# One block and one product for the last 64 query rows of two head groups, without the idle products between stages

## The chip, the cores and the metric

The kernel runs on one core of a Trainium2 chip. The metric is the device time of one execution in microseconds (us). Three runs of the kernel before took 212.29, 211.98 and 211.97 us, so its median is 211.98 us. One further execution was profiled.

## The reference, cut to what matters

Four rows `x` of 448 numbers pass a decode step of attention over a window of 1024 cached positions, and then a small mixer:

```
q = (layernorm(x) @ wq)               # wq: 448 x 4096, 16 query heads of 256, 8 key/value heads
p = softmax(q @ k^T / 16)             # k, v: 4 x 8 x 1024 x 256 of the caches
h = x + (p @ v) @ wo                  # wo: 4096 x 448
y = layernorm(layernorm(h))
out = h + gelu(y @ w1 + b1) @ w2 + b2 # w1: 448 x 1792, w2: 1792 x 448
```

All is float32. Caches and weights are each read once, some 88 MB. The change touches the query projection `layernorm(x) @ wq`: its contraction over 448 rows is three blocks of 128 rows and a last one of 64.

## The kernel before, in words

A *group* is one key/value head with its two query heads (512 columns of `wq`); there are eight groups, handled in four pairs. The host packs everything that a stage needs into one array of 128 partitions, and one long load brings it into a slot. There are three slots, used in turn: the slots hold `wq0` and `k0` (one slot), then `l1` to `l8`, then the end (`k7`, `vo`, `v7`, `wo`, `w1`, `w2`). All loads are issued by SyncE (SP) in program order. A load into a slot waits for the last reader of the part that it overwrites, so SP stands between loads and waits for TensorE (PE). `Machine.emit` (lines 131 to 177) writes the waits out: all operations are recorded by one helper, line 74, so the rows of the profile mostly show line 74 and have to be told apart by tiles.

Names in the rows: `slot` is a slot, `qT`, `pT`, `oT`, `yT`, `gT` are small transposed operands, and `b_s`, `b_o`, `b_m`, `b_t`, `b_acc` are banks of PSUM for scores, values, small products, transposes and the running output. A float32 product shows as two MATMUL instructions, each with its own LDWEIGHTS; a bfloat16 product as one.

For a pair of groups the stages are: `both_queries` (line 493: projection of both groups into `b_m`, then `queries` transposes the result into `qT`), `scores`, `softmax`, `transpose_p`, `values`, `outputs`. The work of one pair is spread over several loads.

The projection, `project` (line 323), takes its parts from `wq_parts` (line 239). Its result is a bank in which quadrant `j` (32 partitions) takes the product with block `j` of the 448 rows; `queries` adds the four quadrants up later. Operand `yT[g]` holds the normalized rows so that group 0 comes out in rows 0 to 3 of a quadrant and group 1 in rows 4 to 7. Blocks 0 to 2 are 128 rows by 512 columns. The last 64 rows of a group are packed as 128 partitions by 256 columns (first half of the columns above, second half below), so quadrant 3 takes two products of half width per group:

```
for i in range(2):
    parts.append((3, y[:, 3 + i, :], slice(i * 2 * P, (i + 1) * 2 * P), t[:, 3 * 512 :]))
```

Group 1 of the first pair is an exception: its last 64 rows come in a tile of their own, `wq1_last` (64 partitions by 512 columns), by two small loads whose source has eight rows of 2 KB times four (lines 463 to 466):

```
for i in range(2):
    nc.sync.dma_start(
        wq1_last[i * Q : (i + 1) * Q, :], wq1[i].rearrange("e (p c) -> e p c", c=512)[:, :4, :]
    )
```

In SP's order they stand behind `wq0` and `k0` and ahead of `l1`.

At the end of seven stages `keep_warm_between` (line 444) issues six products of a tile of zeros, `idle` (bfloat16, 128 x 512), into a bank `b_t` that nothing reads. Similar calls of `keep_warm` stand in the tail, behind `l8`, and stay.

Of the kernel before, what the change touches and what calls it, by code (L numbers as in the profile page):

```python
# [5 lines left out]
F32 = mybir.dt.float32  # L6
# [5 lines left out]
B, D = 4, 448  # L12
HQ, HKV, SK, DH = 16, 8, 4096, 256
# [3 lines left out]
P = 128  # L17
H = P // 2
ND = 4
# [3 lines left out]
Q = 32  # L23
CACHE = NKC * B * DH
HALF = CACHE // 2
WEIGHTS = 4 * D
SLOT = CACHE + 2 * WEIGHTS + HALF
COLUMNS = ND * B + 4 + 4 * 4
EPS = 1e-5
# [2 lines left out]
GRANULE = 4  # L32


class Memory:
# [9 lines left out]
    def part(self, ap):  # L45
        if self.psum:
            return slice(0, 1), np.zeros(1, int)
        pairs = list(ap.ap)
        first, at = divmod(ap.offset, self.row)
        rows = slice(first // GRANULE, -(-(first + pairs[0][1]) // GRANULE))  # L50
        cols = np.zeros(1, int)
        for step, n in pairs[1:]:
            cols = (cols[:, None] + step * np.arange(n)).ravel()
        return rows, np.unique(cols) + at
# [142 lines left out]
        return flat.rearrange(f"p ({names}) -> p {names}", **{f"a{i}": n for i, n in enumerate(shape[1:])})  # L197


def block_kernel(nc, wq0, k0, wq1, l1, l2, l3, l4, l5, l6, l7, l8, k7, vo, v7, wo, w1, w2, out):  # L200
    real, nc = nc, Machine(nc)

    def rows_of_tag(name, shape, dtype):
# [13 lines left out]
    ps_s, ps_t, ps_m = (Pool(bank, 2) for _ in range(3))  # L217
    ps_o, ps_w = (Pool(bank, 1) for _ in range(2))

    def slot(name):  # L220
        return ring.tile([P, SLOT], F32, tag="slot", name=name)

    def load(t, at, src, pieces=None):
        dst = t[:, at : at + src.shape[-1]]
        at = 0
        for n in pieces or (src.shape[-1],):
            nc.sync.dma_start(dst[:, at : at + n], src[:, at : at + n])
            at += n
        return dst

    def cut(t, sizes):
        parts, at = [], 0
        for n in sizes:
            parts.append(t[:, at : at + n])
            at += n
        return parts


    def wq_parts(y, t, last=None):
        parts = [(a, y[:, a, :], slice(0, 512), t[:, a * 512 : (a + 1) * 512]) for a in range(3)]  # L240
        if last is not None:
            return parts + [(3, y[:H, 3, :], slice(0, 512), last)]
        for i in range(2):
            parts.append((3, y[:, 3 + i, :], slice(i * 2 * P, (i + 1) * 2 * P), t[:, 3 * 512 :]))
        return parts


    def keys(t):
# [2 lines left out]
    def chunks(t):  # L251
        v = t.rearrange("p (c b d) -> p c b d", b=B, d=DH)
        return [v[:, c : c + 2] for c in range(0, v.shape[1], 2)]

    def output_weights(t):
# [6 lines left out]
        out=ident, in_=ident, compare_op=ALU.not_equal, fill=1.0, base=0, pattern=[[-1, P]], channel_multiplier=1  # L262
# [9 lines left out]
    nc.vector.tensor_add(sel, sel, ident[:, 3 * Q : 4 * Q])  # L272


    yz = const.tile([P, ND + 1, B + Q], F32, name="yT")
    nc.vector.memset(yz, 0.0)
    yT = [yz[:, :, B:], yz[:, :, :Q]]
    wq1_last = const.tile([H, 512], F32, name="wq1_last")
    zT = const.tile([P, ND, Q], F32, name="zT")
    nc.vector.memset(zT, 0.0)  # L280

# [38 lines left out]
        nc.gpsimd.tensor_tensor(dst, ve, mhalf[: dst.shape[0], : dst.shape[1]], op=ALU.pow)  # L320


    def project(pq, parts, start):
        for j, y, cols, w in parts:
            nc.tensor.matmul(
                pq[j * Q : (j + 1) * Q, cols], y, w,
                start=start and cols.start == 0, stop=not start and cols.stop == 512,
            )

    def pq_tile(n):  # L330
        return ps_m.tile([P, 512], F32, tag="m", name=f"pq{n}")

    def queries(n, pq):
        qs = work.tile([P, 512], F32, tag="qs", name=f"qs{n}")
        nc.scalar.copy(qs, pq)

        pt = ps_m.tile([P, 2 * REP, P], F32, tag="m", name=f"pqt{n}")
        for i in range(2 * REP):
            nc.tensor.transpose(pt[:, i, :], qs[:, i * P : (i + 1) * P], ident)
        sm = work.tile([P, 2 * REP, 2 * B], F32, tag="sm", name=f"sm{n}")  # L340
        nc.vector.tensor_reduce(
            sm, pt.rearrange("p i (j q) -> p i q j", j=4)[:, :, : 2 * B, :], axis=AX.X, op=ALU.add
        )
        for g in range(2):
            src = sm.rearrange("p (r c) b -> p c b r", r=REP)[:, :, g * B : (g + 1) * B, :]
            for i in range(2):
                at = (2 * g + i) * REP
                nc.vector.tensor_copy(qT[g][:, :, :, at : at + REP], src)
# [91 lines left out]
    def keep_warm(n, warm):  # L440
        for _ in range(n):
            nc.tensor.matmul(warm[:Q], idle[:, :Q], idle, start=True, stop=True)

    def keep_warm_between():
        warm = ps_t.tile([P, 512], F32, tag="t", name="between")
        keep_warm(6, warm)

    def po_tile(g, pool=ps_o, tag="o"):
        return pool.tile([P, 2, DH], F32, tag=tag, name=f"po{g}")


    t = slot("t0")
    wqt, xT, b2T, b1T = cut(load(t, 0, wq0), (WEIGHTS, ND * B, 4, 4 * 4))
    wqt = wq_parts(yT[0], wqt)
    xT = xT.rearrange("p (a b) -> p a b", a=ND)
    ka, kb, wqt1 = cut(load(t, WEIGHTS + COLUMNS, k0), (HALF, HALF, 3 * 512))
    for i in range(2):
        nc.sync.dma_start(
            wq1_last[i * Q : (i + 1) * Q, :], wq1[i].rearrange("e (p c) -> e p c", c=512)[:, :4, :]
        )  # L460
    d = work.tile([P, ND, B], F32, tag="d", name="d_x")
    centred(d, xT, "x")
    sx = work.tile([P, ND, B], F32, tag="sx", name="sx")
# [1 line left out]
    rx = work.tile([P, B], F32, tag="rx", name="rx")  # L465
    rsqrt(rx, column_mean(sx, "sx"), "x")
    nc.vector.tensor_mul(yT[0][:, :3, :B], d[:, :3, :], rx[:, None, :].to_broadcast([P, 3, B]))
    nc.vector.tensor_mul(yT[0][:H, 3, :B], d[:H, 3, :], rx[:H, :])
    nc.vector.tensor_mul(yT[0][H:, 4, :B], d[H:, 3, :], rx[H:, :])
    pq = pq_tile(0)  # L470
    project(pq, wqt, True)

    wide = t[:, SLOT - 6 * P :].rearrange("p (n j q) -> p n j q", n=6, j=4)
    nc.vector.tensor_copy(
# [5 lines left out]
    for at, n in ((0, 2), (2 * P, 4)):  # L480
# [3 lines left out]
        cols = min(n * P, rs.shape[1] - at)  # L484
        nc.scalar.copy(rs[:, at : at + cols], pr.rearrange("p i c -> p (i c)")[:, :cols])

    project(pq, wq_parts(yT[1], wqt1, wq1_last), False)
    queries(0, pq)
    s = score_tiles(0)
    for h, kt in enumerate((ka, kb)):  # L490
# [2 lines left out]
    def both_queries(n, wqs):  # L493
        pq = pq_tile(n)
        for g in range(2):
            project(pq, wq_parts(yT[g], wqs[g]), g == 0)
        queries(n, pq)

    def outputs(n, po, rec, wos):
        transposed_output(n, po, rec, range(2))  # L500
        for g in range(2):
            add_output(n, g, output_weights(wos[g]))

    ka, kb, va = cut(load(slot("l1"), 0, l1), (HALF, HALF, HALF))
    for h, kt in enumerate((ka, kb)):
        scores(s, 1, h, keys(kt))
    p, sums = softmax(0, s)
    rec = transpose_p(0, p, sums)
    po = po_tile(0)
    values(0, chunks(va), po, range(0, 2))  # L510
    keep_warm_between()

    vb, v, wo_a, wo_b = cut(load(slot("l2"), 0, l2), (HALF, CACHE, WEIGHTS, WEIGHTS))
    values(0, chunks(va) + chunks(vb), po, range(2, 4))
    values(1, chunks(v), po)
    outputs(0, po, rec, (wo_a, wo_b))
    keep_warm_between()

    wq_a, wq_b, ka, kb, k2 = cut(load(slot("l3"), 0, l3), (WEIGHTS, WEIGHTS, HALF, HALF, HALF))
    both_queries(1, (wq_a, wq_b))  # L520
    s = score_tiles(1)
    for h, kt in enumerate((ka, kb)):
        scores(s, 0, h, keys(kt))
    scores(s, 1, 0, keys(k2))
    keep_warm_between()

    k2, v, wq_a, wq_b = cut(load(slot("l4"), 0, l4), (HALF, CACHE, WEIGHTS, WEIGHTS))
    scores(s, 1, 1, keys(k2))
    p, sums = softmax(1, s)
    both_queries(2, (wq_a, wq_b))  # L530
    rec = transpose_p(1, p, sums)
    po = po_tile(1)
    values(0, chunks(v), po)
    keep_warm_between()

    v, wo_a, wo_b, ka = cut(load(slot("l5"), 0, l5), (CACHE, WEIGHTS, WEIGHTS, HALF))
    values(1, chunks(v), po)
    s = score_tiles(2)
    scores(s, 0, 0, keys(ka))
    outputs(1, po, rec, (wo_a, wo_b))  # L540
    keep_warm_between()

    kb, ka, k2 = cut(load(slot("l6"), 0, l6), (HALF, HALF, HALF))
    scores(s, 0, 1, keys(kb))
# [1 line left out]
        scores(s, 1, h, keys(kt))  # L546
    p, sums = softmax(2, s)
    rec = transpose_p(2, p, sums)
    keep_warm_between()

    v, va, wq_a, wq_b = cut(load(slot("l7"), 0, l7), (CACHE, HALF, WEIGHTS, WEIGHTS))
    po = po_tile(2)
    values(0, chunks(v), po)
    values(1, chunks(va), po, range(0, 2))
    both_queries(3, (wq_a, wq_b))
    keep_warm_between()

    vb, wo_a, wo_b, ka, kb = cut(load(slot("l8"), 0, l8), (HALF, WEIGHTS, WEIGHTS, HALF, HALF))
    values(1, chunks(va) + chunks(vb), po, range(2, 4))
# [6 lines left out]
    e = [slot(f"te{i}") for i in range(3)]  # L566
    kt = [keys(t) for t in cut(load(e[0], 0, k7), (HALF, HALF))]
    v, wot = cut(load(e[1], 0, vo), (CACHE, 2 * D))
# [9 lines left out]
    p, sums = softmax(3, s)  # L578
# [14 lines left out]
    warm = ps_t.tile([P, 512], F32, tag="t", name="warm")  # L593
# [8 lines left out]
    last = ps_s.tile([P, 512], F32, tag="s", name="last")[:, :P]  # L602
# [38 lines left out]
    d = once.tile([P, P], F32, tag="dh", name="dh")  # L641
# [28 lines left out]
    for a in (0, 1, 3, 2):  # L670
        m = Q if a == 0 else B
        for j in range(4):
            rows, w = w1_part(a, j)
# [23 lines left out]
    first = 8  # L697
    pa = ps_w.tile([P, D], F32, tag="acc", name="pa")
    for c in range(first):
        j, m = c % 4, Q if c < 4 else B  # L700
# [95 lines left out]
```

## Time and profile before

| | before |
|---|---|
| median of three runs | 211.98 us |
| profiled execution, its own time | 212.03 us |
| its span, first to last instruction | 210.7 us |
| PE busy, instructions | 138.5 us, 976 MATMUL and 976 LDWEIGHTS |
| bytes moved | 88.42 MB |
| mean granted TensorE clock | 0.862 of full speed |

The span is 1.33 us shorter than the execution's own time. A page of the profile gives busy time by engine, the DMA queues, and the chain of work that ended last, followed back from the last instruction. "A <- B" in a wait means that A's engine stood idle until B was done. The view of windows gives, for a stretch of the span, the busy time of each engine with its number of instructions, the mean granted clock of TensorE (1.00 is 2.4 GHz, 0.50 is 1.2 GHz) and the busy share of the 16 DMA engines. In short stretches that share can pass 1.

### The profile page before, as it was taken

The numbers are of one execution on the slowest core, as the hardware profiler recorded it, in microseconds if no ns is written. First come the engines' busy times: TensorE is split into PE (matmuls) and PEld (weight loads), VectorE is DVE, ScalarE is ACT, GpSimd is POOL, SyncE is SP. The second block draws the span as 40 slices with busy tenths as digits, with TensorE's granted clock in tenths as the row PEclk, the third lists the DMA queues.
The fourth block names the chain that finished last, engine by engine and source line by source line (L and its number), as shares of the span: only waits on it lengthen the run. The fifth ranks groups of instructions, "written<-read, shape, count | busy, mean of one in ns | idle before, by whom it ended". The sixth has DMA issues, their size and how long they took to land.

```text
span 210.7 us, 2189 instructions
## 1 busy us (share of the span) xinstructions
PE 138.5 (66%) x976; PEld 47.2 (22%) x976; DVE 28.8 (14%) x135; ACT 14.4 (7%) x34; POOL 5.0 (2%) x17
## 2 busy tenths in 40 slices
PE   0557869621971676098459577619806999888996
PEld 0420212200220221023112111202301223224332
DVE  7210101300020011013002003200100213012320
ACT  2010000200000010011000000200100002010311
POOL 5100000000000000000000000000000000000100
PEclk9999996985697599769969958757975899999999
DMA  7999999899999999999999999999999999999993
GB/s 296 428 399 473 448 491 389 386 411 530 398 398 410 530 389 410 410 518 398 413 411 448 481 398 437 398 494 398 446 392 448 416 428 429 437 398 452 412 410 131
DMA packets 3256, 88.42 MB, mean 420 GB/s; under 512 B 368, under 2 KB 624, under 8 KB 1200
## 3 DMA queue, kind: packets, MB, share of 16 engines
q1 hardware_dynamic: 3248, 88.30, 97.5%
q8 instruction: 7, 0.11, 0.2%
q14 instruction: 1, 0.01, 0.0%
HBM read 88.23 MB, written 0.07 MB: 419 GB/s over the span
## 4 chain that ended last, share of the span: by engine, by line
DMA 78%; PE 17%; SPq 2%; DVE 1%; issue 1%; ACT 0%
DMA slot<-l 64%; DMA slot<-w 14%; PE b_o L74 9%; PE b_s L74 4%; PE b_acc L74 3%; SPq L74 2%; PE b_m L74 1%; DVE oT L74 1%; DVE w_o L74 0%; PE b_t L74 0%; DVE o_u L74 0%; ACT o_u L74 0%; DVE o_res L74 0%
## 5 line engine op out<-in xcount | busy, mean ns | idle before, releaser
L74 PE MATMUL b_o<-slot,pT 128*32 128x512 f32 x224 | 32.3, 729 | 26.3 <-DMA slot<-l 25.6
L74 PE MATMUL b_s<-slot,qT 128*32 128x512 f32 x256 | 38.7, 760 | 14.3 <-DMA slot<-l 12.9
L74 PE MATMUL b_m<-slot,yT 128*32 128x512 f32 (+1 forms) x76 | 11.4, 705 | 11.4 <-DMA slot<-l 6.2
L74 PEld LDWEIGHTS b_s<-slot,qT 128*32 128x32 f32 x256 | 9.4, 136 | 40.8 <-issue 23.9
L74 PEld LDWEIGHTS b_o<-slot,pT 128*32 128x32 f32 x224 | 7.7, 130 | 47.5 <-DMA slot<-l 28.0
L74 PE MATMUL b_t<-idle 128*32 128x512 bf16 x64 | 17.7, 397 | 0.5 <-DVE pT L74 0.5
L74 DVE TENSOR_REDUCE w_mx<-b_s 128x1 f32<-128x512 f32 x8 | 5.5, 691 | 49.5 <-PE b_s L74 49.5
L74 ACT ACTIVATE o_p<-b_s,w_nm 128x512 f32<-128x512 f32 x8 | 5.4, 682 | 96.4 <-DVE w_nm L74 96.4
L74 DVE TENSOR_SCALAR w_o<-b_o,w_rec 128x512 f32<-128x512 f32 x4 | 3.0, 751 | 50.2 <-PE b_o L74 50.2
L74 PEld LDWEIGHTS b_m<-slot,yT 128*32 128x32 f32 x76 | 4.2, 140 | 17.8 <-DMA slot<-l 6.7
L74 PEld LDWEIGHTS b_t<-idle 128*32 128x32 bf16 x64 | 5.9, 99 | 9.9 <-issue 5.2
L74 PE MATMUL b_t<-ident,o_p 128*128 128x128 f32 x32 | 5.0, 283 | 4.0 <-ACT o_p L74 3.9
L74 PE MATMUL b_acc<-slot,oT 128*32 128x448 f32 x52 | 6.1, 546 | 1.9 <-DVE oT L74 1.9
L74 DVE TENSOR_REDUCE w_sm<-b_m 128x32 f32<-128x128 f32 x4 | 1.2, 291 | 44.8 <-PE b_m L74 44.8
L74 ACT COPY w_qs<-b_m 128x512 f32<-128x512 f32 x4 | 2.3, 584 | 58.0 <-PE b_m L74 58.0
L74 POOL TENSOR_TENSOR o_r<-w_ve,mhalf 128x1 f32<-128x1 f32 x2 | 1.1, 542 | 189.3 <-DVE w_ve L74 189.3
L74 PEld LDWEIGHTS b_t<-ident,o_p 128*128 128x128 f32 x32 | 3.4, 141 | 7.4 <-ACT o_p L74 7.4
L74 PE MATMUL b_m<-ident,w_qs 128*128 128x128 f32 x16 | 3.1, 324 | 3.0 <-ACT w_qs L74 3.0
L74 PE MATMUL b_m<-slot,mean 128*128 128x12 f32 (+1 forms) x4 | 1.1, 371 | 5.4 <-DMA slot<-wq 5.4
L74 PE MATMUL b_o<-slot,yT 128*32 128x512 f32 x10 | 4.6, 595 | 0.0
L74 PE MATMUL b_m<-ident,w_o 128*128 128x128 f32 x20 | 3.3, 287 | 1.8 <-DVE w_o L74 1.8
L74 DVE COPY pT<-b_t 128x16 f32<-128x16 f32 x32 | 3.3, 167 | 5.9 <-PE b_t L74 5.9
(94 smaller groups left out, 66.3 us busy)
## 6 DMA issues: line engine op xcount, KB each, us to landing
slot<-l SPq DMA_DIRECT2D x6, 7936.0 KB, 43.7
slot<-l SPq DMA_DIRECT2D x2, 6144.0 KB, 35.3
slot<-k SPq DMA_DIRECT2D x1, 4864.0 KB, 15.7
slot<-vo SPq DMA_DIRECT2D x1, 4544.0 KB, 32.9
slot<-k SPq DMA_DIRECT2D x1, 4096.0 KB, 40.9
slot<-v SPq DMA_DIRECT2D x1, 3072.0 KB, 18.8
slot<-w SPq DMA_DIRECT2D x1, 2240.0 KB, 28.4
slot<-w SPq DMA_DIRECT2D x1, 1792.0 KB, 33.8
```

Source lines behind the costliest of these rows:

```text
L74: self.machine.add(Op(self.name, lambda: getattr(issuer, what)(*args, **kwargs), outs, ins, what))
```

## The change

The last 64 rows of both groups of a pair share one block of 128 partitions by 512 columns: group 0's rows above, group 1's below. One product of full width then serves both groups: the upper half of the operand's chunk 3 carries the normalized rows in the columns of group 0, the lower half in those of group 1. The block comes with the load that holds the first group's weights, for the first pair with `wq0`; the two small loads and their tile are gone. Bytes in all are the same: `wq0` grows by 128 KB, the two small loads of 64 KB each go, and `l3`, `l4`, `l7` keep their size. `keep_warm_between` and its seven calls are gone. A correction in `Memory.part` counts the partitions of an access by their step; it alters no wait of the operations here.

```
-    def wq_parts(y, t, last=None):
-        parts = [(a, y[:, a, :], slice(0, 512), t[:, a * 512 : (a + 1) * 512]) for a in range(3)]
-        if last is not None:
-            return parts + [(3, y[:H, 3, :], slice(0, 512), last)]
-        for i in range(2):
-            parts.append((3, y[:, 3 + i, :], slice(i * 2 * P, (i + 1) * 2 * P), t[:, 3 * 512 :]))
-        return parts
+    def wq_parts(y, t):
+        return [(a, y[:, a, :], t[:, a * 512 : (a + 1) * 512]) for a in range(3)]
+
+    def wq_last(t):
+        return [(3, yT[0][:, 3, :], t)]
...
-    yz = const.tile([P, ND + 1, B + Q], F32, name="yT")
+    yz = const.tile([P, ND, B + Q], F32, name="yT")
...
-    wq1_last = const.tile([H, 512], F32, name="wq1_last")
...
-    def project(pq, parts, start):
-        for j, y, cols, w in parts:
-            nc.tensor.matmul(
-                pq[j * Q : (j + 1) * Q, cols], y, w,
-                start=start and cols.start == 0, stop=not start and cols.stop == 512,
-            )
+    def project(pq, parts, start, stop):
+        for j, y, w in parts:
+            nc.tensor.matmul(pq[j * Q : (j + 1) * Q], y, w, start=start, stop=stop)
...
-    def keep_warm_between():
-        warm = ps_t.tile([P, 512], F32, tag="t", name="between")
-        keep_warm(6, warm)
...
-    wqt, xT, b2T, b1T = cut(load(t, 0, wq0), (WEIGHTS, ND * B, 4, 4 * 4))
-    wqt = wq_parts(yT[0], wqt)
+    wqt, wq_both, xT, b2T, b1T = cut(load(t, 0, wq0), (QUERY, 512, ND * B, 4, 4 * 4))
     xT = xT.rearrange("p (a b) -> p a b", a=ND)
-    ka, kb, wqt1 = cut(load(t, WEIGHTS + COLUMNS, k0), (HALF, HALF, 3 * 512))
-    for i in range(2):
-        nc.sync.dma_start(
-            wq1_last[i * Q : (i + 1) * Q, :], wq1[i].rearrange("e (p c) -> e p c", c=512)[:, :4, :]
-        )
+    ka, kb, wqt1 = cut(load(t, QUERY + 512 + COLUMNS, k0), (HALF, HALF, QUERY))
...
-    nc.vector.tensor_mul(yT[0][H:, 4, :B], d[H:, 3, :], rx[H:, :])
+    nc.vector.tensor_mul(yT[0][H:, 3, B : 2 * B], d[H:, 3, :], rx[H:, :])
     pq = pq_tile(0)
-    project(pq, wqt, True)
+    project(pq, wq_parts(yT[0], wqt), True, False)
+    project(pq, wq_last(wq_both), True, True)
...
-    project(pq, wq_parts(yT[1], wqt1, wq1_last), False)
+    project(pq, wq_parts(yT[1], wqt1), False, True)
...
         for g in range(2):
-            project(pq, wq_parts(yT[g], wqs[g]), g == 0)
+            project(pq, wq_parts(yT[g], wqs[g]), g == 0, g == 1)
+        project(pq, wq_last(wqs[2]), True, True)
         queries(n, pq)
...
-    keep_warm_between()
```

The last line stands for the seven calls behind the work of `l1` to `l7`.

## Rows read from the trace of the kernel before

**Rows 1.** The page: span, busy time by engine, DMA bytes and queues.

```profile
span 210.7 us, 2189 instructions
...
PE 138.5 (66%) x976; PEld 47.2 (22%) x976; DVE 28.8 (14%) x135; ACT 14.4 (7%) x34; POOL 5.0 (2%) x17
...
q1 hardware_dynamic: 3248, 88.30, 97.5%
q8 instruction: 7, 0.11, 0.2%
```

**Rows 2.** The chain that ended last: start, length, what.

```profile
170.25 28.45 DMA slot<-w
...
198.83 3.48 PE b_s L74 x32
```

**Rows 3.** Timeline of the tail: start, length, engine, operation, idle before and releaser.

```profile
180.50 3.64 PE L74 MATMUL b_o<-slot,pT 128*32 128x512 f32 x32 [0.54 <-DMA slot<-vo]
...
206.73 0.56 PEld L74 LDWEIGHTS b_o<-slot,gT 128*32 128x32 f32 x24 [0.63 <-DMA slot<-w]
...
208.34 0.11 PEld L74 LDWEIGHTS b_o<-slot,gT_last 128*4 128x4 f32 x8 [0.21 <-DMA slot<-w]
208.81 0.29 DVE L74 TENSOR_TENSOR o_res<-b_o,o_hb 128x128 f32<-128x128 f32 x1 [4.40 <-PE b_o L74]
```

**Rows 4.** Groups by form: all idle products, and the small loads' issues on SP's timeline.

```profile
L74 PE MATMUL b_t<-idle 128*32 128x512 bf16 x64 | 17.7, 397 | 0.5 <-DVE pT L74 0.5
...
1.64 1.55 SPq L74 DMA_DIRECT2D wq_last<-wq  x2
...
168.93 0.80 SPq L74 DMA_DIRECT2D slot<-v  x2
```

**Rows 5.** Windows: us, busy by engine (instructions), clock, DMA share, GB/s.

```profile
107.90:120.00 12.10, 10.23 (x74) 3.04 (x74) 1.35 (x5) 0.00 (x0) 0.00 (x0) 0.89 0.98 424
...
141.10:152.80 11.70, 10.86 (x78) 3.55 (x78) 0.70 (x5) 0.58 (x1) 0.00 (x0) 0.84 1.00 434
152.80:159.90 7.10, 0.01 (x1) 0.01 (x2) 0.00 (x0) 0.00 (x0) 0.00 (x0) 0.65 0.94 406
159.90:167.00 7.10, 6.84 (x36) 1.80 (x36) 0.94 (x3) 0.00 (x0) 0.00 (x0) 0.63 1.02 436
167.00:180.00 13.00, 12.56 (x82) 3.85 (x82) 3.08 (x16) 1.45 (x4) 0.00 (x0) 1.00 0.99 426
```

**Rows 6.** Timeline of PE, columns as in Rows 3: first stage, stage `l7`, start of `l8`.

```profile
16.97 1.93 PE L74 MATMUL b_m<-slot,yT 128*32 128x512 f32 x6 [3.37 <-DMA slot<-k]
...
141.21 7.08 PE L74 MATMUL b_o<-slot,pT 128*32 128x512 f32 x48 [4.78 <-DMA slot<-l]
...
148.12 1.90 PE L74 MATMUL b_m<-slot,yT 128*32 128x512 f32 x20
...
151.32 1.47 PE L74 MATMUL b_t<-idle 128*32 128x512 bf16 x6
...
159.89 3.64 PE L74 MATMUL b_o<-slot,pT 128*32 128x512 f32 x16 [7.10 <-DMA slot<-l]
```

**Rows 7.** DMA packets begun in the windows 15.85 to 16.25, 15.5 to 16.6 and 15.7 to 17.0.

```profile
DMA packets 35, 0.14 MB, mean 359 GB/s; under 512 B 11, under 2 KB 11, under 8 KB 33
...
DMA packets 89, 0.56 MB, mean 505 GB/s; under 512 B 25, under 2 KB 25, under 8 KB 80
...
DMA packets 112, 0.92 MB, mean 706 GB/s; under 512 B 32, under 2 KB 32, under 8 KB 96
```

**Rows 8.** Windows, columns as in Rows 5, at the end of the stream.

```profile
204.00:205.80 1.80, 1.73 (x17) 0.79 (x20) 0.21 (x1) 0.32 (x2) 0.00 (x0) 1.00 0.95 389
...
206.60:207.20 0.60, 0.60 (x24) 0.47 (x22) 0.00 (x0) 0.22 (x1) 0.00 (x0) 1.00 0.53 212
207.20:207.60 0.40, 0.40 (x20) 0.13 (x8) 0.00 (x0) 0.31 (x1) 0.00 (x0) 1.00 0.46 175
```

**Rows 9.** DMA queues in the window 200 to 210.7: packets, MB, share of 16 engines.

```profile
q8 instruction: 1, 0.02, 0.5%
```

More of the change, by code (lines that the diff above doesn't have):

```diff
@@ L26 @@
 WEIGHTS = 4 * D
+QUERY = 3 * 512
 SLOT = CACHE + 2 * WEIGHTS + HALF
@@ L49, in part @@
         first, at = divmod(ap.offset, self.row)
-        rows = slice(first // GRANULE, -(-(first + pairs[0][1]) // GRANULE))
+        end = first + pairs[0][0] // self.row * (pairs[0][1] - 1) + 1
+        rows = slice(first // GRANULE, -(-end // GRANULE))
         cols = np.zeros(1, int)
@@ L197, in tile, with block_kernel @@
         return flat.rearrange(f"p ({names}) -> p {names}", **{f"a{i}": n for i, n in enumerate(shape[1:])})
-def block_kernel(nc, wq0, k0, wq1, l1, l2, l3, l4, l5, l6, l7, l8, k7, vo, v7, wo, w1, w2, out):
+def block_kernel(nc, wq0, k0, l1, l2, l3, l4, l5, l6, l7, l8, k7, vo, v7, wo, w1, w2, out):
     real, nc = nc, Machine(nc)
@@ L516, in block_kernel @@
     outputs(0, po, rec, (wo_a, wo_b))
-    keep_warm_between()
-    wq_a, wq_b, ka, kb, k2 = cut(load(slot("l3"), 0, l3), (WEIGHTS, WEIGHTS, HALF, HALF, HALF))
-    both_queries(1, (wq_a, wq_b))
+    wq_a, wq_b, wq_c, ka, kb, k2 = cut(load(slot("l3"), 0, l3), (QUERY, QUERY, 512, HALF, HALF, HALF))
+    both_queries(1, (wq_a, wq_b, wq_c))
     s = score_tiles(1)
@@ L524, in block_kernel @@
     scores(s, 1, 0, keys(k2))
-    keep_warm_between()
-    k2, v, wq_a, wq_b = cut(load(slot("l4"), 0, l4), (HALF, CACHE, WEIGHTS, WEIGHTS))
+    k2, v, wq_a, wq_b, wq_c = cut(load(slot("l4"), 0, l4), (HALF, CACHE, QUERY, QUERY, 512))
     scores(s, 1, 1, keys(k2))
     p, sums = softmax(1, s)
-    both_queries(2, (wq_a, wq_b))
+    both_queries(2, (wq_a, wq_b, wq_c))
     rec = transpose_p(1, p, sums)
@@ L533, in block_kernel @@
     values(0, chunks(v), po)
-    keep_warm_between()
     v, wo_a, wo_b, ka = cut(load(slot("l5"), 0, l5), (CACHE, WEIGHTS, WEIGHTS, HALF))
@@ L540, in block_kernel @@
     outputs(1, po, rec, (wo_a, wo_b))
-    keep_warm_between()
     kb, ka, k2 = cut(load(slot("l6"), 0, l6), (HALF, HALF, HALF))
@@ L548, in block_kernel @@
     rec = transpose_p(2, p, sums)
-    keep_warm_between()
-    v, va, wq_a, wq_b = cut(load(slot("l7"), 0, l7), (CACHE, HALF, WEIGHTS, WEIGHTS))
+    v, va, wq_a, wq_b, wq_c = cut(load(slot("l7"), 0, l7), (CACHE, HALF, QUERY, QUERY, 512))
     po = po_tile(2)
@@ L554, in block_kernel @@
     values(1, chunks(va), po, range(0, 2))
-    both_queries(3, (wq_a, wq_b))
-    keep_warm_between()
+    both_queries(3, (wq_a, wq_b, wq_c))
     vb, wo_a, wo_b, ka, kb = cut(load(slot("l8"), 0, l8), (HALF, WEIGHTS, WEIGHTS, HALF, HALF))
@@ L745, in packed @@
         return np.concatenate([full, last], axis=-1)
-    wq = packed(np.asarray(A_wq).reshape(D, HKV, 512).transpose(1, 0, 2))
+    wq = np.asarray(A_wq).reshape(D, HKV // 2, 2, 512)
+    whole = wq[: 3 * P].reshape(3, P, HKV // 2, 2, 512).transpose(2, 3, 1, 0, 4).reshape(HKV, P, QUERY)
+    last = wq[3 * P :].transpose(1, 2, 0, 3).reshape(HKV // 2, P, 512)
+    wq = [np.concatenate([whole[2 * n], whole[2 * n + 1], last[n]], axis=1) for n in range(HKV // 2)]
     wo = np.asarray(A_wo).reshape(HKV, 4, P, D).transpose(0, 2, 1, 3).reshape(HKV, P, 4 * D)
@@ L753 @@
         (vb[0], v[1], wo[0], wo[1]),
-        (wq[2], wq[3], k[2], ka[3]),
-        (kb[3], v[2], wq[4], wq[5]),
+        (wq[1], k[2], ka[3]),
+        (kb[3], v[2], wq[2]),
         (v[3], wo[2], wo[3], ka[4]),
         (kb[4], k[5]),
-        (v[4], va[5], wq[6], wq[7]),
+        (v[4], va[5], wq[3]),
         (vb[5], wo[4], wo[5], k[6]),
@@ L761 @@
     loads = {f"l{i + 1}": np.concatenate(parts, axis=1) for i, parts in enumerate(loads)}
-    k0 = np.concatenate([k[0], wq[1][:, : 3 * 512]], axis=1)
-    wq1 = np.asarray(A_wq).reshape(D, HKV, 512)[3 * P :, 1].reshape(2, 8, 4 * 512)
-    wq1 = np.concatenate([wq1, np.zeros((2, 8, 512), np.float32)], axis=2)
+    k0 = np.concatenate([k[0], whole[1]], axis=1)
     vo = np.concatenate([v[6], wo[6, :, : 2 * D]], axis=1)
@@ L782 @@
     arrays = {
-        "wq0": np.concatenate([wq[0], xT, b2, b1], axis=1), "k0": k0, "wq1": wq1, **loads, "k7": k[7], "vo": vo, "v7": v[7], "wo": wo_end, "w1": w1, "w2": w2,
+        "wq0": np.concatenate([whole[0], last[0], xT, b2, b1], axis=1), "k0": k0, **loads, "k7": k[7], "vo": vo, "v7": v[7], "wo": wo_end, "w1": w1, "w2": w2,
     }
```

## The prediction

> **What bounds the kernel now.** I read the page's totals first. PE is busy for 138.5 of 210.7 us, but the queue of loads keeps the 16 DMA engines busy for 97.5% of the span [rows 1]: 88.30 MB over 16 engines in 0.975 x 210.7 = 205.4 us is 26.9 KB per us and engine. The chain of waits says the same at its end: the load of `w1` and `w2` holds it for 28.45 us until 198.7 [rows 2]. The reader should look next at how late the stream itself runs. In the last microseconds PE still stops for pieces of `w2`, at 206.73 and at 208.34 [rows 3], 0.47 us before the final addition. So the time is: start, stream, about half a microsecond of products, output. PE had stood idle for only 0.21 us before 208.34 [rows 3]; it follows closely, and a stream that ended more than about 0.2 us earlier would not give all of that back.
>
> Thus an edit on PE counts only if it delays a load's issue or the work behind the last landings, and an edit of the loads counts in full if it moves the last engine of the sixteen.
>
> **The parts of the change.** *Idle products.* Of the 64 idle products [rows 4] 42 go (seven sets of six), the 22 in the tail stay. A set takes 1.47 us [rows 6] and lies at the end of a stage; behind it PE waits for the next landing, 7.10 us in stage `l8` [rows 6] and 4.78 in `l7`. Removing it only makes that wait longer: gain zero. What it may cost is the clock. With the products in place the granted clock already was 0.65 in the gap before `l8` and 0.63 in its first 7.1 us [rows 5], so that stage starts largely at the lower level (1.2 GHz) either way. A ceiling for the others: stage `l7` has 10.86 us of PE work at clock 0.84 [rows 5], of it 1.47 idle products; the rest wholly at 0.50 would be 9.39 x 0.84 / 0.50 = 15.8 us, and the next landing is 159.89 - 141.21 = 18.7 us behind [rows 6]. The stage of `l5` (107.9 to 120, 10.23 us at 0.89 [rows 5]) comes to 15.6 us in the same way, 1.1 more than the 14.5 until `l6` lands, and the stage behind it has room.
>
> What SP then issues late: loads wait for released slots. The tightest is `v7`, issued at 168.93 [rows 4] when the work on `l8` is done, with `vo` ahead of it in the queue until PE receives that at 180.50 [rows 3]: 11.5 us of cover. If the 6.84 us of work at 0.63 [rows 5] ran wholly at 0.50 it would take 1.8 us more. Behind `v7` SP holds `wo`, `w1` and `w2`; all would come 1.8 us later and still in time. Cost zero; if the cover were gone, 1.8 us.
>
> The Trainium skill speaks against this removal ("TensorE: Matmul & The Clock Gate", section "Why this matters for your kernels"): gaps of idle TensorE between bursts drop the clock and should be avoided. The trace agrees that the clock drops in the gaps, and shows that it did so with the products too [rows 5]; by that rule the stages get longer, and by the rows that length is hidden everywhere but in the tail.
>
> *The projection.* A call of `both_queries` shows 20 MATMULs [rows 6]: ten products of two passes. It becomes seven products, 14 MATMULs. In the first pair nine products become seven. Together 18 + 4 = 22 MATMULs and as many weight loads fewer, some 2 us, all in stages that end in a wait for a landing. Zero. The first pair's last block now needs only `wq0`; its other products still wait for `k0` until 16.97, after 3.37 us of idling [rows 6], which also covers that `wq0` lands some 0.3 us later, being 128 KB longer (8 KB on each of 16 engines at 26.9 KB/us = 0.30).
>
> *SP.* Two issues go, 1.55 us [rows 4], so `l1` and `l2` are issued that much earlier, behind a queue that has `k0` to move until 16.6. Zero.
>
> *The stream.* The bytes stay. What moves is who carries 128 KB: before, the small loads put it on eight engines, 16 KB each, 0.61 us; after, all sixteen take 8 KB, 0.30 us. So eight engines gain 0.30 us and eight lose 0.30, and what counts is which half holds the last engine. The small packets tell something [rows 7]. Counting those under 8 KB without those under 512 B: 64 in all (15.7 to 17.0), of which 22 had begun by 16.25 and 55 by 16.6, while PE still waited for `k0` until 16.97. So the eight engines that take them are through with `k0` before most of the others, by about what the small loads cost: the others begin `l1` directly (long packets: two by 16.25, nine by 16.6), the last of these eight between 16.6 and 17.0. The small loads filled a lead of those engines. After the change the lead is unfilled: these begin `l1` about 0.3 us earlier, the others 0.30 later, the last of them at about 16.9. The last engine at that point is as late as before: change 0.
>
> The engines do not stay together, though. At the end half of them are done by 206.6, and the share stays near one half until 207.6 [rows 8]; the later half is over 1 us behind, more than the small loads could make. Instruction packets come to about that: seven of 16 KB [rows 1], one of them 0.5% of 16 engines over 10.7 us = 0.86 us on its one engine [rows 9]. So the last engine is one that carried such a packet. If the seven fall without a plan on sixteen engines, some will fall among those that now come 0.30 later. The change of the end is between 0 (a small-load engine was last before, another is as late now) and +0.30 (a late one of the others was last); from below it is bounded by -0.30 (only small-load engines carried them). I take +0.2, nearer to the upper end, because [rows 7] show most of the others beginning `l1` together, seven of nine between 16.25 and 16.6, where one of seven packets would hardly miss all.
>
> **Sum.** Against the profiled execution: 212.03 + 0 + 0 + 0 + 0.2 = 212.23 us. The median of the runs is 0.05 us lower, so 212.2 us. A measurement of this kernel can tell from no change about 0.2%, 0.42 us: 211.56 to 212.40 is "the same".
>
> **Rivals.** *The small-load engines were the last.* Then the last engine gains 0.30 us, a little more with the small loads' own overhead. For it: the last to begin `l1` is one of them [rows 7]. Against it: only half of the engines took them, and the packets of instructions would all have to fall there. PE's slack of 0.21 us [rows 3] clips it: 0.2 to 0.35 us, 211.6 to 211.8. The Trainium skill has this as a rule ("DMA: Bandwidth & Descriptors", section "Rules for kernel authors"): small transfers should be merged into large ones and spread over all 16 engines; by that the sum would be this rival's. The rows show the uneven split, but no loss from it.
>
> *One instruction packet fewer, on the engine that ended last.* 42 + 22 MATMULs with their weight loads are 128 of 1952 instructions on PE; seven packets times 128/1952 is about half a packet. The last one may vanish or fall behind the stream. Gain 0.86 us: 211.1. Against it: eight engines are equally late [rows 8], so freeing one gives nothing.
>
> *Slower: two instruction packets on one engine.* With PE's program shortened, the packets come at other moments, and if one hits an engine that already carried one, that engine ends the stream 0.86 us later still, and `w2` with it: 212.9, with the 0.2 above 213.1. It decides from the second packet on one engine onwards. For it: seven packets, sixteen engines, and the ends of [rows 8] show about one packet each. Against it: they fell apart before.
>
> *Half clock in the tail.* If the clock that rose to 1.00 at 167 [rows 5] did not, the 3.48 us of `w1` products at 198.83 [rows 2] would take twice that: 215.4. Against it: the gap before `l8` was at the low clock already.
>
> **How the numbers follow.** The forecast 0.62, of which 0.54 lies within 0.2%, 0.06 above (+0.3 and some overhead) and 0.02 below. Small-load engines last 0.16 (0.13 within, 0.03 faster). One packet fewer 0.08 (0.07 faster, 0.01 within). Two on one engine 0.10, half clock 0.04, both slower. Faster 0.12, the same 0.68, slower 0.20. The range reaches from the first rival's lower end, 211.6, to the lower end of the two packets, 212.9; it leaves out the fewer packet, the half clock and half of the two packets, some 0.17.
>
> **What the profile after would show.** Right: DMA share full until 206, the last landing that PE waits for at 208.3 to 208.6, gaps before landings longer by about 1.5 us with a clock near 0.5 in them, `v7` issued before 171. Wrong: `v7` issued past 178, a clock below 1.00 behind 180, an end of the stream before 207.9 or after 209, or PE idle for long in the tail without a landing as its releaser.

## The result, and the profile after

The kernel after takes 212.74 us (median of eight runs, 212.48 to 213.05), the kernel before 212.06 in as many runs beside it (211.94 to 212.29). The ratio is 1.0032, with an interval of 1.0023 to 1.0041: slower by 0.68 us. That lies within the range of the prediction, but past the 0.2% (0.42 us) up to which it had called the time the same. The execution profiled after took 212.77 us.

The page of the kernel after, in the parts that answer to [rows 1]:

```profile
span 211.5 us, 2062 instructions
...
PE 126.7 (60%) x912; PEld 41.1 (19%) x912; DVE 28.8 (14%) x135; ACT 14.4 (7%) x34; POOL 5.0 (2%) x17
...
q1 hardware_dynamic: 3168, 88.30, 97.3%
q8 instruction: 7, 0.11, 0.2%
```

PE has 64 MATMULs fewer, 42 idle products and 22 of the projection, and is busy for 11.8 us less. The span is 0.8 us longer all the same. The bytes of the loads are those of before, 88.30 MB. The queue's share times the span says how long an engine was busy with them: 0.973 x 211.5 = 205.8 us, before 205.4. So the engines took about 0.4 us longer over the same bytes (each product is rounded to some 0.1 us); the other 0.4 us an average engine stood idle, as those do that are done before the last one.

The chain that ended last (start, length, what) shows the end of the loads and nothing new behind it. Before, it left the loads at 198.7 for the products of `w1` [rows 2]; now it stays with them until 205.74, when a piece of `w2` lands:

```profile
171.20 34.54 DMA slot<-w
205.74 0.14 issue
205.88 1.71 PE b_acc L76 x16
207.59 1.96 PE b_o L76 x38
209.54 0.02 issue
209.57 0.29 DVE o_res L76
```

The timeline of the kernel after (start, length, engine, operation, in brackets the idle time before and its releaser) shows where the time was lost; compare [rows 3] and [rows 6]:

```profile
17.33 1.26 PE L76 MATMUL b_m<-slot,yT 128*32 128x512 f32 x6 [3.16 <-DMA slot<-k]
...
51.70 7.26 PE L76 MATMUL b_o<-slot,pT 128*32 128x512 f32 x48 [9.54 <-DMA slot<-l]
70.46 3.63 PE L76 MATMUL b_m<-slot,yT 128*32 128x512 f32 x14 [7.77 <-DMA slot<-l]
...
89.48 3.64 PE L76 MATMUL b_s<-slot,qT 128*32 128x512 f32 x16 [6.12 <-DMA slot<-l]
...
141.52 6.74 PE L76 MATMUL b_o<-slot,pT 128*32 128x512 f32 x48 [8.50 <-DMA slot<-l]
160.27 3.64 PE L76 MATMUL b_o<-slot,pT 128*32 128x512 f32 x16 [8.93 <-DMA slot<-l]
181.03 3.64 PE L76 MATMUL b_o<-slot,pT 128*32 128x512 f32 x32 [1.07 <-DMA slot<-vo]
199.40 3.44 PE L76 MATMUL b_s<-slot,zT 128*32 128x448 f32 x32 [0.24 <-DMA slot<-w]
...
209.10 0.11 PEld L76 LDWEIGHTS b_o<-slot,gT_last 128*4 128x4 f32 x8 [0.24 <-DMA slot<-w]
209.57 0.29 DVE L76 TENSOR_TENSOR o_res<-b_o,o_hb 128x128 f32<-128x128 f32 x1 [4.59 <-PE b_o L76]
```

The landings of `l2`, `l3` and `l4` in the kernel before, for comparison:

```profile
51.70 7.46 PE L74 MATMUL b_o<-slot,pT 128*32 128x512 f32 x48 [8.26 <-DMA slot<-l]
...
70.40 3.22 PE L74 MATMUL b_m<-slot,yT 128*32 128x512 f32 x20 [6.24 <-DMA slot<-l]
...
89.22 3.64 PE L74 MATMUL b_s<-slot,qT 128*32 128x512 f32 x16 [6.92 <-DMA slot<-l]
```

Read the starts from top to bottom against those of before. `k0` comes 0.36 us later (17.33 against 16.97), because `wq0` ahead of it is longer. At `l2` (51.70) both kernels are level to 0.01 us, at `l3` 0.06 apart. From there the lag grows, in unequal pieces: 0.26 at `l4`, 0.31 at `l7`, 0.38 at `l8`, 0.53 at `vo`, 0.57 at `w1`, 0.76 at the last piece of `w2` and at the final addition. No single wait was added: the landings fall behind over the whole stream from `l3` on, and PE waits for every one of them.

In the windows (us, busy time by engine, clock, DMA share, GB/s) the stream's end has its old shape, only later; compare [rows 8]:

```profile
206.60:207.20 0.60, 0.60 (x12) 0.13 (x4) 0.00 (x0) 0.00 (x0) 0.00 (x0) 1.00 0.53 209
207.20:207.60 0.40, 0.40 (x14) 0.16 (x11) 0.00 (x0) 0.00 (x0) 0.00 (x0) 1.00 0.57 216
...
208.00:208.40 0.40, 0.40 (x19) 0.17 (x10) 0.00 (x0) 0.17 (x1) 0.00 (x0) 1.00 0.29 108
```

About half of the engines are through soon after 206.6; the late half now runs past 208.

### The profile page after: what moved, and what is told of

Its sections match the earlier page's. It is cut to its first block, busy times and chain, and to the rows that moved or that the text cites. A ratio compares the mean times of both kernels' runs of the same rounds, so it can differ in the third digit from the quotient of the medians.

```text
span 211.5 us, 2062 instructions
## 1 busy us (share of the span) xinstructions
PE 126.7 (60%) x912; PEld 41.1 (19%) x912; DVE 28.8 (14%) x135; ACT 14.4 (7%) x34; POOL 5.0 (2%) x17
## 3 DMA queue, kind: packets, MB, share of 16 engines
q1 hardware_dynamic: 3168, 88.30, 97.3%
## 4 chain that ended last, share of the span: by engine, by line
DMA 81%; PE 15%; SPq 2%; DVE 1%; issue 1%
DMA slot<-l 64%; DMA slot<-w 16%; PE b_o L76 9%; PE b_acc L76 3%; PE b_s L76 2%; SPq L76 2%; PE b_m L76 1%; DVE oT L76 1%; DVE w_o L76 0%; DVE o_res L76 0%
## 5 line engine op out<-in xcount | busy, mean ns | idle before, releaser
L76 PE MATMUL b_o<-slot,pT 128*32 128x512 f32 x224 | 33.1, 745 | 35.0 <-DMA slot<-l 33.8
L76 PE MATMUL b_s<-slot,qT 128*32 128x512 f32 x256 | 37.9, 745 | 16.5 <-DMA slot<-l 15.2
L76 PE MATMUL b_m<-slot,yT 128*32 128x512 f32 x56 | 11.0, 798 | 12.7 <-DMA slot<-l 7.8
L76 PE MATMUL b_t<-idle 128*32 128x512 bf16 x22 | 6.6, 382 | 0.0
L76 PEld LDWEIGHTS b_m<-slot,yT 128*32 128x32 f32 x56 | 2.3, 134 | 18.6 <-DMA slot<-l 8.6
L76 PEld LDWEIGHTS b_m<-ident,w_qs 128*128 128x128 f32 x16 | 2.3, 179 | 8.0 <-ACT w_qs L76 8.0
```

Of the source, the lines that this page charges most:

```text
L76: self.machine.add(Op(self.name, lambda: getattr(issuer, what)(*args, **kwargs), outs, ins, what))
```

## The experiments

Every ratio is to the kernel before, run on the same chip, whose median was 212.04 to 212.07 us. Diffs start from the kernel after or the kernel before, as each says. At first there were two theories for the 0.68 us: the *balance* of the 128 KB (eight engines or sixteen, the prediction's term) and the *idle products* with their clock; instruction packets came in as a third. A fourth, the *addresses* into which the loads write, was formed when these had fallen.

**The idle products, back in the kernel after.**

```
+    def keep_warm_between():
+        warm = ps_t.tile([P, 512], F32, tag="t", name="between")
+        keep_warm(6, warm)
...
+    keep_warm_between()      # at the end of the same seven stages
```

> The changed kernel with the seven sets of six idle products put back; the loads stay as changed. Theory (loads): the small loads had filled a lead of about 0.3 us that eight of the sixteen DMA engines have after the first two loads; without them the other eight carry 0.30 us more each, and instruction packets of some 0.9 us fall on those. Then this kernel is as slow as the changed one: 212.7 us, ratio to the kernel before 1.003, last pieces of w2 awaited past 208.8. Rival (products): the missing idle products, by the clock or by the moments of the instruction packets, cost the time: 212.1 us, ratio 1.000.

Measured: 212.79 us, 1.0034 (1.0021 to 1.0047). The 42 products are back and the loss stays whole.

**The idle products gone from the kernel before**, nothing else changed.

```
-    keep_warm_between()      # all seven, and the function
```

> The kernel before without its seven sets of idle products, nothing else; the small loads on eight engines stay. Theory (loads): 212.1 us, ratio 1.000 within 0.001, with a mean clock as low as in the changed kernel (0.83) and PE's gaps longer by about 1.5 us. Rival (products): 212.7 us, ratio 1.003.

Measured: 212.03 us, 0.9998 (0.9989 to 1.0008). The mean granted clock of its profile is 0.830, before 0.862, and it costs nothing. Its timeline has `l8` and the end where the kernel before has them [rows 3, 6]:

```profile
159.91 3.64 PE L74 MATMUL b_o<-slot,pT 128*32 128x512 f32 x16 [7.74 <-DMA slot<-l]
...
208.34 0.11 PEld L74 LDWEIGHTS b_o<-slot,gT_last 128*4 128x4 f32 x8 [0.20 <-DMA slot<-w]
208.81 0.29 DVE L74 TENSOR_TENSOR o_res<-b_o,o_hb 128x128 f32<-128x128 f32 x1 [4.38 <-PE b_o L74]
```

The two runs settle that part from both sides.

**The small loads kept**, in the kernel after: group 0's 64 rows of the first pair are loaded alone, the other 64 by the two small loads.

```
-    wqt, wq_both, xT, b2T, b1T = cut(load(t, 0, wq0), (QUERY, 512, ND * B, 4, 4 * 4))
+    wqt, xT, b2T, b1T = cut(load(t, 0, wq0), (QUERY, ND * B, 4, 4 * 4))
+    nc.sync.dma_start(both[:H, :], last0)
...
+    for i in range(2):
+        nc.sync.dma_start(
+            both[H + i * Q : H + (i + 1) * Q, :], wq1[i].rearrange("e (p c) -> e p c", c=512)[:, :4, :]
+        )
```

> The changed kernel with one block and one product for both groups, but the first pair's block is loaded apart: group 0's 64 rows by a load over all sixteen engines, group 1's 64 rows by the two small loads over eight, behind k0 as in the kernel before. Theory (loads): all of the loss comes back, 212.1 us, ratio 1.000, although products and program are the changed kernel's. Rival (products): 212.7 us, ratio 1.003.

Measured: 214.54 us, 1.0122 (1.0108 to 1.0136), 1.8 us more than the kernel after and far from both numbers. It was to isolate the small loads and did not: the edit has a price of its own, and all of it falls at the start. The timeline has `k0` awaited 1.22 us later than in the kernel after and, by 34.10, `l1` 2.2 us later; from there the lag does not grow.

```profile
18.55 1.93 PE L76 MATMUL b_m<-slot,yT 128*32 128x512 f32 x6 [4.79 <-DMA slot<-k]
34.10 5.07 PE L76 MATMUL b_s<-slot,qT 128*32 128x512 f32 x32 [3.32 <-DMA slot<-l]
```

Which of its three loads costs this was not separated. The kernel before has the two small loads behind `k0` too, and `k0` lands at 16.97 there, so the suspicion falls on the one ahead of `k0`. On the balance it says nothing.

**Two small loads once more**, in the kernel after: 128 KB on eight engines into a tile of which only one column is copied, to nothing that counts.

```
+    spare = const.tile([H, 512], F32, name="spare")
+    seen = const.tile([H, 1], F32, name="seen")
...
+    for i in range(2):
+        nc.sync.dma_start(
+            spare[i * Q : (i + 1) * Q, :], wq1[i].rearrange("e (p c) -> e p c", c=512)[:, :4, :]
+        )
...
+    nc.vector.tensor_copy(seen, spare[:, :1])
```

> The changed kernel with the two small loads added once more, into a tile of which one column is read and not used: 128 KB more, all on eight engines (16 KB, 0.61 us each). Theory (loads): these eight are ahead at the end, so 0.61 us more on each costs nothing: 212.7 us, ratio to the changed kernel 1.000, although 128 KB more are moved. Rival (any engine can be the last one): the end comes 0.3 to 0.6 us later, 213.0 to 213.3 us.

Measured: 212.72 us, 1.0037 (1.0024 to 1.0050).

**The same 128 KB over all sixteen engines**, in the kernel after.

```
+    spare = const.tile([P, 256], F32, name="spare")
+    seen = const.tile([P, 1], F32, name="seen")
...
+    nc.sync.dma_start(spare, wq1)      # 128 x 256
...
+    nc.vector.tensor_copy(seen, spare[:, :1])
```

> The changed kernel with 128 KB more in one load over all sixteen engines behind k0 (256 columns for 128 partitions, one column read and not used): the same additional bytes as in the run with the small loads added once more. Theory (loads): every engine takes 8 KB more, the last ones too, so the end comes 0.30 us later: 213.0 us, where the same bytes on eight engines cost nothing. Rival (bytes count alike wherever they go): both runs the same, 212.7 us or both 213.0 us.

Measured: 212.76 us, 1.0031 (1.0019 to 1.0043), not the 213.0 of the theory. Eight engines or sixteen: by the ratios the two runs lie 0.06% apart (0.13 us), well within their intervals. If the late engines were all of one half, the load on eight would have cost either nothing or twice the other.

**The small loads' bytes spread, in the kernel before**: packed into `wq0`, so they come over sixteen engines; its two products of half width stay.

```
-    wqt, xT, b2T, b1T = cut(load(t, 0, wq0), (WEIGHTS, ND * B, 4, 4 * 4))
+    wqt, wq1_last, xT, b2T, b1T = cut(load(t, 0, wq0), (WEIGHTS, 2 * P, ND * B, 4, 4 * 4))
...
-    for i in range(2):
-        nc.sync.dma_start(
-            wq1_last[i * Q : (i + 1) * Q, :], wq1[i].rearrange("e (p c) -> e p c", c=512)[:, :4, :]
-        )
```

> The kernel before, idle products and half-width products as they were; only the last 64 rows of group 1 of the first pair, which the small loads brought over eight engines, now come packed like all others inside wq0, over sixteen. Theory (loads): this alone makes the whole loss, 212.7 us, ratio 1.003. Rival (the one block and its product add something of their own): 212.1 to 212.4 us.

Measured: 212.10 us, 1.0003 (0.9994 to 1.0012). This is the change's move of bytes alone, and it costs 0.03 us. Its timeline: `k0` late by 0.40 us as in the kernel after, `l8` as early as before.

```profile
17.37 1.93 PE L74 MATMUL b_m<-slot,yT 128*32 128x512 f32 x10 [3.43 <-DMA slot<-k]
...
159.84 3.64 PE L74 MATMUL b_o<-slot,pT 128*32 128x512 f32 x16 [6.89 <-DMA slot<-l]
```

**More by small loads**, in the kernel before without its idle products: group 0's last 64 rows also come over the eight engines.

```
+    for n, last in enumerate((wq1_last, wq0_last)):
+        for i in range(2):
+            nc.sync.dma_start(
+                last[i * Q : (i + 1) * Q, :], wq1[n, i].rearrange("e (p c) -> e p c", c=512)[:, :4, :]
+            )
...
```

> The kernel before without its idle products, and with the last 64 rows of group 0 of the first pair too taken out of wq0 and brought by two small loads over the eight engines (into partitions 0 to 63). The other eight engines carry 0.30 us less than in the kernel before, these eight 0.30 us more. Theory (loads): the last engine is still one of the others, so the time falls by up to 0.30 us below the kernel before: 211.75 us, ratio 0.9985. Rival (the small loads had just balanced the engines): 212.4 us, slower than before.

Measured: 212.29 us (211.76 to 212.94), 1.0013 (1.0004 to 1.0022). More on the eight does not gain 0.30 us, it loses 0.22 us, on the rival's side. With these runs the theory of the balance falls.

**More instruction packets**, in the kernel after: 1500 memsets on POOL, which is idle there, into a tile that nothing reads.

```
+    pads = const.tile([P, 1500], BF16, name="pads")
...
+    for i in range(1500):
+        nc.gpsimd.memset(pads[:, i : i + 1], 0.0)
```

> The changed kernel with 1500 small memsets on POOL, of columns that nobody reads, from about 24 us on: POOL has no other work until the tail. If POOL's instructions come in packets of 16 KB like PE's, there are several more of them on the queue of instructions. Theory (instruction packets set the last engine apart): more engines are late, the DMA share between 207.4 and 208.2 us rises from about 0.4 towards 0.8, and the end comes later by up to 1.4 us where an engine gets a second packet: 212.7 to 214.1 us. Rival (instruction packets are too small to matter): share and time unchanged, 212.7 us.

Measured: 219.04 us, 1.0329 (1.0315 to 1.0343): 6.3 us more than the kernel after, and more than either side had foreseen. Its page gives POOL's memsets as a group (line, engine, operation; busy time and mean ns; idle before) and twelve packets more than the kernel after in the queue of POOL's instructions:

```profile
q14 instruction: 13, 0.11, 0.1%
...
L76 POOL MEMSET pads<- 128x1 bf16 x1500 | 50.2, 101 | 13.7 <-issue 13.7
```

The delay came while POOL was fetching: between its memsets, 128 at a time, it pauses for 0.9 to 1.8 us. `l3` lands 6.97 us later than in the kernel after (70.46); the memsets end at 74, and between `l3` and `l8` there is no further delay. The windows show whose it is: behind 208.5, where the other engines are done, the DMA share stays near 1/16, one engine.

```profile
72.39 1.58 POOL L76 MEMSET pads<- 128x1 bf16 x46 [1.05 <-issue]
...
77.43 3.63 PE L76 MATMUL b_m<-slot,yT 128*32 128x512 f32 x14 [9.47 <-DMA slot<-l]
...
166.78 3.64 PE L76 MATMUL b_o<-slot,pT 128*32 128x512 f32 x16 [7.39 <-DMA slot<-l]
```

```profile
208.00:208.50 0.50, 0.50 (x8) 0.11 (x8) 0.00 (x0) 0.00 (x0) 0.00 (x0) 1.00 0.26 97
208.50:210.00 1.50, 1.50 (x12) 0.39 (x4) 0.72 (x2) 0.20 (x1) 0.00 (x0) 1.00 0.05 19
210.00:212.00 2.00, 1.79 (x14) 1.15 (x13) 0.30 (x2) 0.80 (x4) 0.00 (x0) 1.00 0.06 27
```

So packets of instructions can set the end; that these twelve went to one engine is inferred from that share, since the trace does not name the engines. They are not what the change did, as far as their number goes: it stayed as it was, seven and one.

**The addresses.** What is left is a side effect that no line of the diff names. The operand tile `yz` lost a chunk: 4 x 36 x 4 = 576 bytes per partition where it had 720. The program places its tiles one behind the other, each from a multiple of 32 bytes, so the room of `yz` shrinks by 160 bytes, from 736 to 576. The other lost tile, `wq1_last`, takes 2048 bytes with it. Everything behind them moves down by 2208 bytes, the three slots too, and 2208 is 32 more than a multiple of 64. All three slots begin at 0 modulo 64 bytes before and at 32 after. The starts of 36 and 4 that an expectation below gives for the third slot are not those of the program: between the second slot and the third lie five tiles of 8, 4, 4096, 8 and 4 bytes, which take 4224 = 66 x 64 with their rounding, so the third begins as the second does.

**The kernel before, 32 bytes up**: one tile of 32 bytes ahead of the slots that nothing uses, no other edit. Starts: 32, 32, 32.

```
+    const.tile([P, 8], F32, name="pad")
     t = slot("t0")
```

> The kernel before with the same unused tile of 32 bytes ahead of the slots, nothing else, so that the first two slots begin at 32 modulo 64. Theory (addresses): it loses what the changed kernel lost, 212.7 us, ratio 1.003. Rival: 212.1 us, unchanged.

Measured: 212.65 us (212.53 to 212.82), 1.0027 (1.0016 to 1.0038). This is the decisive run. It has the products, the loads and the idle products of the kernel before, and it loses 0.61 us. The profiled execution took 212.82 us. Its timeline has the kernel after's late landings:

```profile
160.14 3.64 PE L74 MATMUL b_o<-slot,pT 128*32 128x512 f32 x16 [7.13 <-DMA slot<-l]
...
180.74 3.64 PE L74 MATMUL b_o<-slot,pT 128*32 128x512 f32 x32 [0.53 <-DMA slot<-vo]
...
199.35 3.44 PE L74 MATMUL b_s<-slot,zT 128*32 128x448 f32 x32 [0.24 <-DMA slot<-w]
...
209.14 0.11 PEld L74 LDWEIGHTS b_o<-slot,gT_last 128*4 128x4 f32 x8 [0.24 <-DMA slot<-w]
209.61 0.29 DVE L74 TENSOR_TENSOR o_res<-b_o,o_hb 128x128 f32<-128x128 f32 x1 [4.69 <-PE b_o L74]
```

**The kernel after, 32 bytes up**, by the same tile: starts 0, 0, 0, as before the change.

> The changed kernel with one unused tile of 32 bytes per partition allocated just ahead of the three slots, nothing else. Theory (addresses): in all kernels that lost 0.7 us or more (the changed one, the one with the products back, the one with the block loaded apart) the first two slots begin at an address that is 32 modulo 64, because the operand tile shrank from 720 to 576 bytes; in the kernel before and in those that lost nothing they begin at 0 modulo 64. Then this pad alone gives the loss back: 212.1 us, ratio to the kernel before 1.000, and packets of 63488 bytes at a median of 2342 ns instead of 2345. Rival (the one block's product or its loads cost something): 212.7 us, unchanged.

Measured: 212.39 us, 1.0022 (1.0012 to 1.0032), with runs from 212.11 to 213.11. About half of the loss comes back by the medians, but the interval overlaps that of the kernel after (1.0023 to 1.0041), so the times alone do not make it certain. The median of the packets came out as the theory had it, 2342 ns. In the timeline, of an execution that took 212.23 us, the landings are again those of the kernel before up to `w1` (159.89 and 198.83 there), 0.2 us late at the last piece:

```profile
159.93 3.64 PE L76 MATMUL b_o<-slot,pT 128*32 128x512 f32 x16 [8.72 <-DMA slot<-l]
...
198.86 3.44 PE L76 MATMUL b_s<-slot,zT 128*32 128x448 f32 x32 [0.32 <-DMA slot<-w]
...
208.55 0.11 PEld L76 LDWEIGHTS b_o<-slot,gT_last 128*4 128x4 f32 x8 [0.24 <-DMA slot<-w]
```

**The kernel after, 64 bytes up**, by a tile of `[P, 16]`: everything moves, and the starts modulo 64 stay 32, 32, 32.

> The changed kernel with an unused tile of 64 bytes ahead of the slots: the slots move, but stay at 32 modulo 64. Theory (addresses modulo 64): 212.7 us, ratio 1.003, as without it. Rival (any shift, or an address modulo a larger number): 212.1 us.

Measured: 212.88 us, 1.0040 (1.0028 to 1.0053): nothing comes back. Moving the tiles as such does not help here.

**All three slots one behind the other**, in the kernel after: the tile of 32 bytes, and no small tiles between the slots. Starts: 0, 0, 0, which the tile alone had given them already.

```
+    const.tile([P, 8], F32, name="pad")
+    for n in range(3):
+        slot(f"s{n}")
     t = slot("t0")
```

> The changed kernel with the 32 byte tile and all three slots allocated one behind the other, so that the third too begins at 0 modulo 64 (it begins at 36 modulo 64 in the kernel before, at 4 in the changed one). Theory (addresses): at least as good as with the 32 bytes alone, 212.0 us; if loads into the third slot were slowed in the kernel before as well, up to 0.3 us below it, 211.8 us. Rival: 212.7 us.

Measured: 212.68 us, 1.0031 (1.0019 to 1.0043). A miss, and one that counts against the theory: the starts modulo 64 are those of the run with the tile alone and of the kernel before, and the loss is whole. `l3` and `l8` land as in the kernel before, 32 bytes up (70.46 and 160.14):

```profile
70.47 3.63 PE L76 MATMUL b_m<-slot,yT 128*32 128x512 f32 x14 [6.75 <-DMA slot<-l]
...
160.22 3.52 PE L76 MATMUL b_o<-slot,pT 128*32 128x512 f32 x16 [7.90 <-DMA slot<-l]
```

What differs from the run with the tile alone is where the small tiles lie that stood between the slots, and how far apart the slots are.

All of it in one table. The fourth column is the time from the landing of `l3` to that of `l8` as PE receives them in each timeline, a stretch that carries the same five loads in every kernel. The fifth is the median time of the 768 DMA packets of 63488 bytes (one partition of a full slot each) that the trace records, the last the start of the final addition. These three come from one profiled execution per kernel, which took between 0.16 us less and 0.45 us more than the median.

| kernel | slot starts modulo 64 | median us | `l3` to `l8` us | packet ns | final addition at us |
|---|---|---|---|---|---|
| before | 0, 0, 0 | 212.06 | 89.49 | 2342 | 208.81 |
| before, idle products gone | 0, 0, 0 | 212.03 | 89.49 | 2342 | 208.81 |
| before, bytes spread | 0, 0, 0 | 212.10 | 89.45 | 2342 | 208.93 |
| before, more on eight | 0, 0, 0 | 212.29 | 89.35 | 2342 | 209.00 |
| after, 32 up | 0, 0, 0 | 212.39 | 89.54 | 2342 | 209.02 |
| after, extra on eight | 0, 0, 0 | 212.72 | 89.42 | 2342 | 209.87 |
| after, extra on sixteen | 0, 0, 0 | 212.76 | 89.56 | 2342 | 209.66 |
| after, slots one behind the other | 0, 0, 0 | 212.68 | 89.75 | 2345 | 209.38 |
| after | 32, 32, 32 | 212.74 | 89.81 | 2345 | 209.57 |
| after, idle products back | 32, 32, 32 | 212.79 | 89.77 | 2345 | 209.58 |
| after, 64 up | 32, 32, 32 | 212.88 | 89.74 | 2345 | 209.93 |
| before, 32 up | 32, 32, 32 | 212.65 | 89.68 | 2345 | 209.61 |
| after, small loads kept | 32, 32, 32 | 214.54 | 89.53 | 2346 | 211.19 |
| after, more packets | 32, 32, 32 | 219.04 | 89.35 | 2345 | 215.97 |

Seven of the eight kernels at 0 take 89.35 to 89.56 us for the stretch, with packets of 2342 ns; the eighth takes 89.75, with 2345. Of the six at 32 four take 89.68 to 89.81, and two, which had lost time ahead of the stretch, 89.53 and 89.35; all six have the slower packets. So the starts modulo 64 sort thirteen of the fourteen kernels by their packets and eleven by the stretch. All eight at 0 are at 0 modulo 128 as well, so 64 and 128 cannot be told apart.

Nor is a start of 32 slow by itself: in the kernel after and in "before, 32 up" the packets of `l1` and `l2` have the same medians as in the kernel before (1815 and 2342 ns), though their slots had moved too; the slower ones come from `l3` or `l4` on. And 3 ns on each of an engine's 48 packets of this size (768 on 16 engines) make some 0.14 us by estimate, a part of the 0.61 only.

The extra tiles of the two runs with 128 KB more had moved the slots back to 0 modulo 64 without my meaning it. So they are to be compared with the 212.39 of "after, 32 up". The difference, 0.33 us on eight engines and 0.37 on sixteen, is near the 0.30 us that 8 KB more on each engine should take, but the intervals of the ratios overlap.

## Why the prediction was right or wrong

**Idle products: zero, right.** Both runs of them agree, and the cover that was named holds. `v7` is issued at 168.93 in the kernel after too, and `l7` and `l8` are waited for longer (8.50 and 8.93 us). The granted clock in the gap before `l8` was 0.63 in the kernel after, 0.65 before [rows 5]. The rule of the Trainium skill ("TensorE: Matmul & The Clock Gate", section "Why this matters for your kernels") agrees with the trace in that the mean clock falls without the products (0.862 to 0.830). What it warns of does not reach the time here, since every stage with such a gap waits for a load.

**Projection and SP: zero, as far as the runs tell.** The 22 products are gone, and PE's waits grow instead. `wq0`'s extra 0.3 us showed as 0.36 at `k0` and was gone by `l2`. Whether the one wide product costs anything in another way is not excluded: it is among what is left of the loss in "after, 32 up".

**The stream: the step that failed.** "The bytes stay. What moves is who carries 128 KB" left out where the bytes go to. The term was +0.2 us by balance; the balance measured 0.03 us, on the run that spreads the bytes in the kernel before. The argument from the small packets [rows 7] to one half of the engines was not borne out, nor was its upper bound of +0.30 for the whole term. That the late half of the engines are those that carried a packet of instructions was not tested. In the place of the term the runs show the place of tiles: 32 bytes more ahead of the slots, with nothing else changed, cost 0.61 us in the kernel before. That this is also what cost the 0.68 us in the kernel after is shown in part only, by the 0.35 us that came back there. The sign was right by accident.

**The rivals.** None of them came. *Small-load engines last* would have made the spreading of the bytes a gain: it was 0.03 us slower, with an interval that ends at a gain of 0.06% (0.13 us), under the rival's 0.2. The rule of the Trainium skill cited with it ("DMA: Bandwidth & Descriptors", section "Rules for kernel authors"), to merge small transfers and spread them, brought nothing here. *One packet fewer* and *two packets on one engine*: the packets stayed seven, and the kernel before with 32 bytes more, with no instruction changed, shows nearly the whole loss. *Half clock in the tail*: the products of `w1` take 3.44 us as before.

**Chances and signs.** The text named an end of the stream after 209 as what would make it wrong, and the last piece of `w2` was awaited until 209.10, past the 208.3 to 208.6 that would have been right. Of the other signs `v7` before 171 came. The waits before `l7` and `l8` grew by 3.7 and 1.8 us, not by about 1.5, at a clock of 0.63 before `l8`, not near 0.5. The range held the time because it had been stretched to a rival that did not happen: that is luck.

**What stays open.** How a move of 32 bytes slows the loads is not shown, only that it does and that the delay spreads over the stream. The tile moves the slots and every tile behind them at once, so it is not shown either that the slots are what matters. Which places are good isn't known: modulo 64 is a description that the run with the slots one behind the other contradicts. Of the loss, undoing the 32 bytes in the kernel after returned 0.35 us, not clear of noise; the other 0.3 us may be the wide product, the other tiles that moved, or scatter of its runs. No version tried beats the kernel before.

## What to carry to other kernels

In a kernel that the loads bound, a tile whose size changes anywhere ahead of the load buffers is part of the change: list what moves, and run the old kernel with a small unused tile in that place before reasons are looked for in the edit. Work taken off an engine that waits for loads bought nothing here, 11.8 us of PE. Instructions added to an idle engine are not free either where their fetches share the DMA engines with the loads: 1500 memsets cost 6.3 us.

## What the runs showed of the hardware that was not expected

- The place of tiles is worth 0.3%: 32 bytes more ahead of the slots took the kernel before from 212.04 to 212.65 us, and its packets of 63488 bytes from 2342 to 2345 ns. A start at 0 modulo 64 is not enough to avoid it (212.68 us with all three slots there).
- Instruction fetches can hold up one of sixteen DMA engines for longer than their bytes would take: 12 packets with some 0.1 MB in all are 3.7 us at the 26.9 KB per us and engine of the prediction (an estimate), and `l3` landed 7 us later. The Trainium skill ("Runtime: NRT & Kernel Launch", section "Instruction fetch mechanics") calls the cost of a refill mostly hidden; with the DMA engines full of loads, as here, it was not.
- A load of 64 partitions and two small ones among the first loads made the kernel after 1.8 us slower, and the delay stayed to the end; which of the three did it was not separated.
